# Half of one output-projection weight per layer to partitions 0 to 63, and a column of ones with step 0

## The chip, the cores and the metric

The kernel runs on one core of one Trainium2 chip. The metric is device time in microseconds, the median of several executions. A profiled execution is at hand too: its times, in us from the first instruction, are what "the profile" and "the trace" mean below.

The core's engines are PE (matrix multiply; PEld is its weight load), DVE (vector), ACT (scalar), POOL and SP. In this kernel all transfers are issued by SP's queue, and 16 DMA engines carry them.

## The reference

Two layers run over one token of width 640, each an attention block and then an MLP block. Attention has 32 heads of width 192 and looks at the last 4096 positions of a cache of keys and values, so that almost all of the bytes are cache. Both layers use the same weights and the same cache.

```python
def _A_ref(x, k_cache, v_cache, wq, wo):
    B, Sq, D = x.shape                     # 1, 1, 640
    Hq, Dh = 32, 192
    Hkv, Sk = k_cache.shape[1], k_cache.shape[2]      # 32, 32768
    W = min(4096, max(256, Sk // 4))                  # 4096
    q = (x @ wq) ...                                  # 32 heads of 192
    k, v = k_cache[:, :, Sk - W:, :], v_cache[:, :, Sk - W:, :]
    scores = einsum("bhqd,bhkd->bhqk", q, k) * Dh ** -0.5
    o = einsum("bhqk,bhkd->bhqd", softmax(scores), v)
    return o (as B, Sq, Hq * Dh) @ wo                 # wo: 6144 x 640

def _B_ref(x, w1, w2, w3, w4):
    hs = 0 for one token (every shifted block reads padding)
    x1 = x + hs
    return x1 + gelu(layernorm(x1) @ w3) @ w4         # 640 -> 1536 -> 640

x = A_x
for layer in range(2):
    x = x + _A_ref(layernorm(x), A_k_cache, A_v_cache, A_wq, A_wo)
    x = x + _B_ref(layernorm(x), B_w1, B_w2, B_w3, B_w4)
```

This is shortened; in the reference the two layers stand written out, and the shift by one or two positions in `_B_ref` is a pad and a slice, which for a sequence of one token leaves zeros.

## The kernel before

**Groups.** The 32 heads form eight groups of four (QH = 4). Layer 0 takes the groups from the last to the first, layer 1 from the first to the last (`GROUPS`). While group gi multiplies probabilities with values (`pv`), the keys of group gi+1 are turned around (`transpose_quart`, L377 on DVE) and scored (`scores`, L453 on PE).

**Transfers.** The big tiles are "cells", NCELL = 11 of them, each 128 partitions of 12,288 bytes: one K or V tile of one head (1536 KB) or one group's `wo` (960 KB). `layer_stream` writes out the order of all transfers for both layers, and `need` issues the next ones on SP's queue until the one asked for is out. So the order is fixed by hand: K and V tiles in turn, the `wo` of a group after its V tiles, at the end of a layer `w3` and `w4`. A transfer waits at SP until its cell is free, and until the eighth transfer before it has landed, as eight semaphores are used in turn. In layer 1 the turned keys of seven heads (NKEEP) and some values are still on chip from layer 0.

**One group's output.** `pv` accumulates a head's output in `O_ps` and DVE transposes it into `o_sb` (L576). `o_fold` sums it over partitions with the fold matrix `Lq` (L583, or L587 and L588 in the middle groups, `add=True`) and ACT scales it with the reciprocal of the softmax sum, `rl`, into the head's 32 partitions of `oT` (L584 or L589). So `oT` is 128 partitions (4 heads x 32) by NA = 6 columns, which is the layout that `load_wo` (L161 to L169) gives the group's rows of `wo`: partition p holds rows 6p to 6p + 5 of that group, one after another. `out_row` (L608) then multiplies `oT` with `wo` as a row: six columns by two halves of 320, L615. Groups at the ends of a layer use `out_proj` (L591, matmuls L597).

**Softmax sums.** `swap` multiplies `lh` with a 128 x 128 matrix of ones (L528, `l_ps`), so that each partition has the sums of the group's four heads; `recip` (L532) picks each partition's own with the mask `blkm` and inverts it. The same matrix of ones forms the sums of the layer norms (L325, L338, L681, L866, L868) and, as one element, of L501.

**Boundary of the layers.** After layer 0's last V tile come the last `pv`, `out_proj`, the norm sums, the products with `w3` (L901) and `w4` (L933), and then layer 1's norm and query projection. The cells that hold the old `w3`, `w4` and V are freed there, and layer 1's first new transfers wait for that.

Of the kernel before, what the change touches and what calls it, by code (L numbers as in the profile page):

```python
# [8 lines left out]
BF16 = mybir.dt.bfloat16  # L9
# [8 lines left out]
P = 128  # L18
# [17 lines left out]
def kernel(  # L36
# [26 lines left out]
    QH = 4  # L63
# [21 lines left out]
    assert W4C % 2 == 1 and W4C < NF  # L85
    GROUPS = [[list(range(h, h + QH)) for h in range(0, H, QH)] for _ in range(2)]
    GROUPS[0].reverse()

    head = ctx.enter_context(tc.tile_pool(name="head", bufs=1))
    fixed = ctx.enter_context(tc.tile_pool(name="fixed", bufs=1))  # L90
# [70 lines left out]
    def load_wo(layer, c):  # L161
        t = take(("wo", layer, c))
        src = A_wo[c * QC:(c + 1) * QC, :].rearrange("(p c) n -> p (c n)", c=NA)
        parts = {NG - 2: (3, 3), NG - 1: (3, 2, 1)}.get(c, (NA,)) if layer == 1 else (NA,)
        i = 0
        for n in parts:
            nc.sync.dma_start(t[:, i * D:(i + n) * D], src[:, i * D:(i + n) * D])
            i += n
        return t  # L169
# [91 lines left out]
        out=ident[:], in_=ident[:], compare_op=ALU.not_equal, fill=1.0,  # L261
        base=0, pattern=[[-1, P]], channel_multiplier=1,
    )
    ones = const.tile([P, P], F32, name="ones")
    nc.vector.memset(ones[:], 1.0)
    Lf = wx_sb[:, 0:2 * P].bitcast(F32).rearrange("p (j i) -> p j i", j=4)
    nc.gpsimd.memset(Lf, 0.0)
    for base in (0, -1, -64, -65):
# [22 lines left out]

    Lq = const.tile([P, 32], F32, name="Lq")
    nc.vector.reduce_sum(Lq[:], ident[:].rearrange("p (j a) -> p a j", j=4), axis=AX.X)
    eps1 = head.tile([P, 1], F32, name="eps1")
    nc.vector.memset(eps1[:], eps)

# [25 lines left out]
    def ln_center(x, rowsum):  # L322

        mean_ps = psm.tile([P, 1], F32, tag="psm")
        nc.tensor.matmul(mean_ps[:], lhsT=ones[:], rhs=rowsum[:, 0:1], start=True, stop=True)  # L325
        xc = big.tile([P, ND], BF16, name="xc")
        nc.vector.scalar_tensor_tensor(out=xc[:], in0=mean_ps[:, 0:1].broadcast_to([P, ND]), scalar=-1.0 / D,
                                       in1=x[:], op0=ALU.mult, op1=ALU.add)
        xcf = big.tile([P, ND], F32, name="xcf")
        nc.vector.scalar_tensor_tensor(out=xcf[:], in0=mean_ps[:, 0:1].broadcast_to([P, ND]), scalar=-1.0 / D,  # L330
                                       in1=x[:], op0=ALU.mult, op1=ALU.add)
        junk = sm.tile([P, ND], F32, tag="ln_junk")
        ssq = sm.tile([P, 1], F32, tag="ln_ssq")
        nc.scalar.activation(junk[:], xcf[:], ACTF.Square, accum_out=ssq[:, 0:1])

        def total():
            var_ps = psm.tile([P, 1], F32, tag="psm")
            nc.tensor.matmul(var_ps[:], lhsT=ones[:], rhs=ssq[:, 0:1], start=True, stop=True)  # L338
            return var_ps

        return xc, xcf, total
# [131 lines left out]
    def softmax_steps(n, ST_ps, sc):  # L473
        held = {}

        def part_max():
            pm = big.tile([P, 1], F32, name="pm")
            nc.vector.tensor_reduce(out=pm[:], in_=ST_ps, op=ALU.max, axis=AX.X)  # L478
            held["pm"] = pm

        def turn_max():
            pmT_ps = psm.tile([1, P], F32, tag="psm")
            nc.tensor.transpose(pmT_ps[0:1, :], held["pm"][:, 0:1], ident[:, :])
            held["pmT"] = pmT_ps

        def full_max():
            ngm = big.tile([1, 2 * QH], F32, name="ngm")
            nc.vector.tensor_reduce(out=ngm[:], in_=held["pmT"][0:1, :].rearrange("o (q x m) -> o x q m", q=4, m=NM),
                                    op=ALU.max, axis=AX.XY, negate=True)
            held["PrT"] = o_bytes[:, SW:2 * SW]  # L490

            wide = held["PrT"][0:1, :].bitcast(F32)
            nc.vector.tensor_scalar(
                out=wide.rearrange("o (q x m) -> o q x m", q=4, m=NM),
                in0=ngm[:].unsqueeze(1).unsqueeze(3).broadcast_to([1, 4, 2 * QH, NM]),
                scalar1=sc[0:1, 0:1], scalar2=None, op0=ALU.mult)
            held["w"] = wide

        def spread_max():
            nb_ps = psm.tile([P, 1], F32, tag="psm")  # L500
            nc.tensor.matmul(nb_ps[:], lhsT=held["w"],  # L501
                             rhs=ones[0:1, 0:1], start=True, stop=True)
            nb_sb = big.tile([P, 1], F32, name="nb_sb")
            nc.scalar.copy(nb_sb[:], nb_ps[:])  # L504
            Pr = o_bytes[:, 0:SW]
            lpart = big.tile([P, 1], F32, name="lpart")
            nc.scalar.activation(out=Pr, in_=ST_ps, func=ACTF.Exp,  # L507
                                 bias=nb_sb[:, 0:1], scale=sc[:, 0:1], accum_out=lpart[:, 0:1])
            held["Pr"], held["l"] = Pr, lpart

        def turn_p():
            nc.vector.transpose(held["PrT"], held["Pr"])  # L512
            lh = big.tile([P, QH], F32, name="lh")
            nc.vector.tensor_scalar(out=lh[:], in0=hm[:], scalar1=held["l"][:, 0:1], scalar2=None, op0=ALU.mult)
            held["lh"] = lh

        def swap():
            ng = NGK // NT
            PT_ps = psm.tile([P, n, NJ4, NGK], F32, tag="psm")
            src = held["PrT"].rearrange("p (g j i) -> p i j g", g=ng, j=NJ4)  # L520
            for m in range(NM):
                for q in range(NT):
                    nc.tensor.matmul(PT_ps[32 * m:32 * (m + 1), :, :, ng * q:ng * (q + 1)], lhsT=Eq[:, q, :],  # L523
                                     rhs=src[:, m:QW:NM], start=True, stop=True)
            PT = big.tile([P, n, NJ4 * NGK], BF16, name="PT")
            nc.scalar.copy(PT[:].rearrange("p h c -> p (h c)"), PT_ps[:].rearrange("p h j g -> p (h j g)"))  # L526
            l_ps = psm.tile([P, QH], F32, tag="psm")
            nc.tensor.matmul(l_ps[:], lhsT=ones[:], rhs=held["lh"][:], start=True, stop=True)  # L528
            held["lps"] = l_ps
            return PT  # L530

        def recip():  # L532
# [5 lines left out]
            return rl  # L538

        return part_max, turn_max, full_max, spread_max, turn_p, swap, recip  # L540

# [18 lines left out]
    def pv(layer, h, hq, PT, mid=None):  # L560
# [17 lines left out]
    def o_fold(h, oT, rl, add=False):  # L578
        r = slice(32 * (h % QH), 32 * (h % QH) + 32)
        oT_ps = psm.tile([P, NA], F32, tag="psm")  # L580
        if not add:
            for e in range(2):
                nc.tensor.matmul(oT_ps[r, :], lhsT=Lq[:], rhs=o_sb[:, e, :, e], start=(e == 0), stop=(e == 1))  # L583
            nc.scalar.activation(oT[r, :], oT_ps[r, :], ACTF.Copy, scale=rl[r, 0:1])  # L584
            return
        o2 = sm.tile([P, NA], F32, name="o2")
        nc.vector.tensor_add(o2[:], o_sb[:, 0, :, 0], o_sb[:, 1, :, 1])  # L587
        nc.tensor.matmul(oT_ps[r, :], lhsT=Lq[:], rhs=o2[:], start=True, stop=True)  # L588
        nc.scalar.activation(oT[r, :], oT_ps[r, :], ACTF.Copy, scale=rl[r, 0:1])  # L589

    def out_proj(layer, *terms):  # L591

# [15 lines left out]
    def out_row(layer, c, oT, acc, first):  # L608
# [1 line left out]
        wo_t = need("wo", layer, c)  # L610
        N = D // 2
        yr_ps = psm.tile([33, N], F32, tag="psm")
        for k in range(NA):
            for i in range(2):
                nc.tensor.matmul(yr_ps[32 * i:32 * i + 1, :], lhsT=oT[:, k:k + 1],  # L615
                                 rhs=wo_t[:, k * D + i * N:k * D + (i + 1) * N], start=(k == 0), stop=(k == NA - 1))
        give(("wo", layer, c))

        def add():
# [21 lines left out]
    def attention(layer, x_cur, rs_cur, x_new, z_new, rs_new, ss_new):  # L641
# [29 lines left out]
        def add_y(y_ps, n):  # L671
            y_new = x_new if n == 0 else sm.tile([P, ND], F32, name="y_acc")
            if n == 1:
# [4 lines left out]

                def center():
                    nm_ps = psm.tile([P, 1], F32, tag="psm")  # L680
                    nc.tensor.matmul(nm_ps[:], lhsT=ones[:], rhs=rs[:, 0:1], start=True, stop=True)  # L681
# [52 lines left out]
        for gi, cur in enumerate(groups):  # L734
            nxt = list(enumerate(groups[gi + 1])) if gi + 1 < len(groups) else []
            ST_n = None
            if nxt:
# [24 lines left out]
                else:  # L762
# [97 lines left out]
    def mixer(layer, x_cur, z, rs_cur, ss_cur, x_new, rs_new):  # L860
# [2 lines left out]


        s1_ps = psm.tile([P, 1], F32, tag="psm")
        nc.tensor.matmul(s1_ps[:], lhsT=ones[:], rhs=rs_cur[:, 0:1], start=True, stop=True)  # L866
        s2_ps = psm.tile([P, 1], F32, tag="psm")
        nc.tensor.matmul(s2_ps[:], lhsT=ones[:], rhs=ss_cur[:, 0:1], start=True, stop=True)  # L868
# [119 lines left out]
```

## Time and profile before

| | us |
|---|---|
| median of 3 runs | 520.23 (519.43 to 520.37) |
| the profiled execution's own time | 519.84 |
| its span, from the first to the last instruction | 518.0 |
| PE busy / DVE busy / ACT busy | 324.8 / 295.2 / 49.5 |
| data read | 216.47 MB, 418 GB/s over the span |

The profile's page gives busy time by engine, the span in 40 slices, the DMA queues, the chain of work that ended last, and the costliest groups of instructions. A group's line reads: source line, engine, operation, out<-in, count, then busy time and mean ns of one, then the idle time before them with what ended it. In the chain and the timeline the first number is the start and the second the length. Besides these answers the trace keeps one record for each DMA packet (queue, start, duration, size).

### The profile page before, as it was taken

Reading aid. Unit: us, or ns where it says so; the run is one execution under the profiler, and the core shown is the slowest. Engines: PE = TensorE matmul, PEld = TensorE weight load, DVE = VectorE, ACT = ScalarE, POOL = GpSimd, SP = SyncE. Lnnn points to the kernel's source line nnn. Section 1 sums busy time; section 2 is a strip of 40 time slices with the busy share of each in tenths; the row PEclk is TensorE's granted clock in tenths of the full one; section 3 lists DMA queues with packets and bytes.
Section 4 is the critical chain, followed back from the end, with each engine's and each line's share of the span. In section 5 each row is a group of like instructions: output and inputs, shape, how many; then the busy total and the mean of one; then the engine's idle time right before and its main releaser. Section 6 shows DMA issues by size and latency. Waiting matters only on the chain.

```text
span 518.0 us, 9589 instructions
## 1 busy us (share of the span) xinstructions
PE 324.8 (63%) x4146; PEld 192.6 (37%) x4146; DVE 295.2 (57%) x589; ACT 49.5 (10%) x175; POOL 4.0 (1%) x16
## 2 busy tenths in 40 slices
PE   2057656666664566767755866777566856648665
PEld 2024334333332334434333634434333433425334
DVE  2067667575584655656624356567675765664722
ACT  1000101010010100001011111001010101001011
POOL 2000000000000000000000000000000000000000
PEclk9999878565586755677665778557785676776855
DMA  8999999999999999999999999999999999999995
GB/s 347 433 425 426 433 426 427 432 428 425 433 426 427 431 426 429 428 426 431 424 425 396 385 426 429 428 428 428 429 426 427 432 428 426 426 434 426 427 416 235
DMA packets 23949, 217.08 MB, mean 419 GB/s; under 512 B 2532, under 2 KB 3044, under 8 KB 8420
## 3 DMA queue, kind: packets, MB, share of 16 engines
q1 hardware_dynamic: 23908, 216.48, 99.0%
q8 instruction: 32, 0.52, 0.4%
q14 instruction: 9, 0.07, 0.0%
HBM read 216.47 MB, written 0.00 MB: 418 GB/s over the span
## 4 chain that ended last, share of the span: by engine, by line
DMA 50%; PE 23%; DVE 22%; issue 2%; ACT 1%; SPq 1%; DVEq 0%; ACTq 0%
DMA cell<-in_A_k_cache_dram 39%; DVE cell L377 16%; DMA cell<-in_A_v_cache_dram 9%; PE ST_ps L453 9%; PE O_ps L569 7%; DVE o_sb L576 2%; DMA cell<-in_B_w_dram 2%; DVE pm L478 1%; PE nb_ps L501 1%; DVE o_sb L512 1%; ACT o_sb L507 1%; PE y_ps L637 1%; PE l_ps L528 1%; PE PT_ps L523 1%; PE qT_ps L407 1%
## 5 line engine op out<-in xcount | busy, mean ns | idle before, releaser
L453 PE MATMUL ST_ps<-cell,Qblk 128*16 128x256 bf16 x1536 | 163.7, 380 | 106.9 <-DVE cell L377 69.4
L377 DVE STREAM_TRANSPOSE cell<-cell 128x768 uint32<-128x768 uint32 x228 | 204.1, 945 | 15.2 <-DMA cell<-in_A_k_cache_dram 14.9
L453 PEld LDWEIGHTS <-Qblk 128*16 128x16 bf16 x1536 | 86.1, 111 | 176.5 <-issue 150.3
L569 PE MATMUL O_ps<-cell,PT 128*2 128x384 bf16 x1018 | 99.9, 461 | 8.2 <-DMA cell<-in_A_v_cache_dram 7.4
L576 DVE STREAM_TRANSPOSE o_sb<-O_ps 128x384 f32<-128x384 f32 x64 | 37.2, 581 | 111.8 <-PE O_ps L569 111.6
L569 PEld LDWEIGHTS <-PT 128*2 128x2 bf16 x1024 | 46.0, 100 | 22.1 <-issue 10.1
L512 DVE STREAM_TRANSPOSE o_sb<-o_sb 128x256 bf16<-128x256 bf16 x16 | 7.1, 446 | 33.2 <-ACT o_sb L507 24.2
L584 ACT ACTIVATE oT<-oT_ps,rl 32x6 bf16<-32x6 f32 x40 | 10.3, 258 | 164.0 <-PE oT_ps L583 157.8
L583 PEld LDWEIGHTS oT_ps<-o_sb,Lq 128*32 128x32 f32 x160 | 13.3, 145 | 19.3 <-issue 15.8
L583 PE MATMUL oT_ps<-o_sb,Lq 128*32 128x6 f32 x160 | 13.9, 195 | 10.4 <-DVE o_sb L576 9.9
L589 ACT ACTIVATE oT<-oT_ps,rl 32x6 bf16<-32x6 f32 x24 | 6.2, 258 | 107.6 <-PE ST_ps L453 87.1
L407 PE MATMUL qT_ps<-xc,wq_sb 128*128 128x1 bf16 x210 | 7.1, 165 | 12.8 <-DMA wq_sb<-in_A_wq_dram 12.0
L523 PE MATMUL PT_ps<-o_sb,Eq 128*32 128x32 bf16 x256 | 7.3, 237 | 9.3 <-DVE o_sb L512 4.1
L523 PEld LDWEIGHTS <-Eq 128*32 128x32 bf16 x256 | 5.4, 108 | 19.8 <-issue 19.7
L421 DVE TENSOR_TENSOR Xq<-qT_ps,maskq 128x24 bf16<-128x24 f32 (+1 forms) x18 | 2.8, 158 | 17.1 <-PE qT_ps L407 17.1
L396 PE MATMUL qr_ps<-wq_sb,xc 128*1 128x384 bf16 x90 | 12.1, 415 | 0.0
L407 PEld LDWEIGHTS <-wq_sb 128*128 128x128 bf16 x210 | 6.7, 102 | 14.0 <-DMA wq_sb<-in_A_wq_dram 13.0
L504 ACT COPY nb_sb<-nb_ps 128x1 f32<-128x1 f32 x16 | 2.5, 159 | 94.6 <-PE nb_ps L501 94.6
L615 PE MATMUL yr_ps<-cell,oT 128*1 128x320 bf16 x108 | 11.2, 355 | 0.0
L528 PE MATMUL l_ps<-lh,ones 128*128 128x4 f32 x32 | 7.7, 310 | 4.9 <-ACT PT L526 4.9
L428 PE MATMUL Qrep_ps<-Xq,Lb 128*128 128x24 bf16 (+1 forms) x18 | 3.2, 178 | 11.1 <-DVE Xq L421 10.8
L588 PE MATMUL oT_ps<-o,Lq 128*32 128x6 f32 x48 | 6.1, 199 | 6.5 <-DVE o L587 6.5
(143 smaller groups left out, 200.9 us busy)
## 6 DMA issues: line engine op xcount, KB each, us to landing
cell<-in_A_k_cache_dram SPq DMA_DIRECT2D x57, 1536.0 KB, 26.3
cell<-in_A_v_cache_dram SPq DMA_DIRECT2D x57, 1536.0 KB, 25.8
cell<-in_A_wo_dram SPq DMA_DIRECT2D x13, 960.0 KB, 26.5
wq_sb<-in_A_wq_dram SPq DMA_DIRECT2D x5, 1536.0 KB, 12.2
cell<-in_A_v_cache_dram SPq DMA_DIRECT2D x4, 768.0 KB, 23.8
cell<-in_A_v_cache_dram SPq DMA_DIRECT2D x2, 1248.0 KB, 11.5
cell<-in_B_w_dram SPq DMA_DIRECT2D x1, 1536.0 KB, 11.9
cell<-in_B_w_dram SPq DMA_DIRECT2D x2, 768.0 KB, 10.3
```

Source lines behind the costliest of these rows:

```text
L377: nc.vector.transpose(Tu, Ku[:, :, q * NY:(q + 1) * NY])
L396: nc.tensor.matmul(qr_ps[32 * i:32 * i + 1, :], lhsT=xc[:, kc:kc + 1], rhs=wq_sb[:, kc, t0 * P + i * N:t0 * P + (i + 1) * N], start=(kc == ...
L407: nc.tensor.matmul(qT_ps[:, tl:tl + 1], lhsT=wq_sb[:, kc, t * P:(t + 1) * P], rhs=xc[:, kc:kc + 1], start=(kc == 0), stop=(kc == ND - 1))
L453: nc.tensor.matmul(ST_ps[r:r + QW, :].rearrange("p (g i) -> p g i", g=ng), lhsT=Q[:, n, :], rhs=T4[:, :, f, :, t], start=(hq == 0 and n == ...
L512: nc.vector.transpose(held["PrT"], held["Pr"])
L523: nc.tensor.matmul(PT_ps[32 * m:32 * (m + 1), :, :, ng * q:ng * (q + 1)], lhsT=Eq[:, q, :], rhs=src[:, m:QW:NM], start=True, stop=True)
L528: nc.tensor.matmul(l_ps[:], lhsT=ones[:], rhs=held["lh"][:], start=True, stop=True)
L569: nc.tensor.matmul(O_ps[r:r + 2, :], lhsT=PT[:, hq, 2 * i:2 * i + 2], rhs=v_pair(V, h, 2 * i * Dh, 2 * Dh), start=(i < 4), stop=(i >= NB - 4))
L576: nc.vector.transpose(o_sb[:], O_ps.rearrange("p (e a c) -> p e c a", e=2, c=NA))
L583: nc.tensor.matmul(oT_ps[r, :], lhsT=Lq[:], rhs=o_sb[:, e, :, e], start=(e == 0), stop=(e == 1))
L584: nc.scalar.activation(oT[r, :], oT_ps[r, :], ACTF.Copy, scale=rl[r, 0:1])
L615: nc.tensor.matmul(yr_ps[32 * i:32 * i + 1, :], lhsT=oT[:, k:k + 1], rhs=wo_t[:, k * D + i * N:k * D + (i + 1) * N], start=(k == 0), stop= ...
```

## The change

In layer 0 the group of heads 16 to 19 and in layer 1 the group of heads 12 to 15 (the fourth in order, `SPLIT`) get their `wo` in another way. Columns 0 to 2 of the six go to 128 partitions as before, 480 KB. Columns 3 to 5, for all 128 rows, go to partitions 0 to 63 only: four transfers of 32 partitions each, 120 KB, two side by side in the free dimension. On the source side the 32 rows are written as 8 x 4, which puts them in another order in the 32 partitions.

`oT` grows to nine columns, the last six with 64 partitions in use. `o_fold_split` writes both parts: columns 0 to 2 with `Lq` to the head's own 32 partitions, columns 3 to 5 with a second fold matrix `Lp` (the new order of rows) to partitions 0 to 31 or 32 to 63. `recip_low` forms the reciprocals that belong to heads 2 and 3 on partitions 0 to 63. `out_row` has nine steps of two matmuls in that group, six of them over 64 partitions.

The matrix of ones becomes one column, read with step 0 along the other dimension.

```diff
+    SPLIT = [GROUPS[layer][3][0] // QH for layer in range(2)]
+    NH = NA // 2
...
     def load_wo(layer, c):
         t = take(("wo", layer, c))
         src = A_wo[c * QC:(c + 1) * QC, :].rearrange("(p c) n -> p (c n)", c=NA)
+        if c == SPLIT[layer]:
+            nc.sync.dma_start(t[:, 0:NH * D], src[:, 0:NH * D])
+            for g in range(4):
+                e = (NH + NH * (g // 2)) * D
+                nc.sync.dma_start(t[32 * (g % 2):32 * (g % 2) + 32, e:e + NH * D],
+                                  src[32 * g:32 * g + 32, NH * D:].rearrange("(b a) n -> a b n", b=4))
+            return t
...
-    ones = const.tile([P, P], F32, name="ones")
-    nc.vector.memset(ones[:], 1.0)
+    one = const.tile([P, 1], F32, name="one")
+    nc.vector.memset(one[:], 1.0)
+    ones = one[:, 0:1].broadcast_to([P, P])
...
+    Lp = const.tile([P, 32], F32, name="Lp")
+    nc.vector.reduce_sum(Lp[:].rearrange("p (a b) -> p a b", b=4),
+                         ident[:].rearrange("p (j b a) -> p a b j", j=4, b=4), axis=AX.X)
...
+        def recip_low():
+            lq = big.tile([P, QH], F32, name="lq")
+            rl = big.tile([P, 1], F32, name="rl_low")
+            nc.vector.scalar_tensor_tensor(out=lq[0:64, 0:2], in0=held["lps"][0:64, 2:4], scalar=1.0,
+                                           in1=blkm[0:64, 0:2], op0=ALU.mult, op1=ALU.mult, accum_out=rl[0:64, 0:1])
+            nc.vector.reciprocal(rl[0:64, :], rl[0:64, :])
+            return rl
...
+    def o_fold_split(h, oT, rl):
+        hq = h % QH
+        r, lo_, e = slice(32 * hq, 32 * hq + 32), slice(32 * (hq % 2), 32 * (hq % 2) + 32), NH + NH * (hq // 2)
+        oT_ps = psm.tile([P, NA + NH], F32, tag="psm")
+        o2 = sm.tile([P, NA], F32, name="o2")
+        nc.vector.tensor_add(o2[:], o_sb[:, 0, :, 0], o_sb[:, 1, :, 1])
+        nc.tensor.matmul(oT_ps[r, 0:NH], lhsT=Lq[:], rhs=o2[:, 0:NH], start=True, stop=True)
+        nc.tensor.matmul(oT_ps[lo_, e:e + NH], lhsT=Lp[:], rhs=o2[:, NH:],
+                         start=True, stop=True)
+        for at, i, s in ((r, 0, rl[0]), (lo_, e, rl[hq // 2])):
+            nc.scalar.activation(oT[at, i:i + NH], oT_ps[at, i:i + NH], ACTF.Copy, scale=s[at, 0:1])
...
     def out_row(layer, c, oT, acc, first):
-        for k in range(NA):
+        split = c == SPLIT[layer]
+        NK = NA + NH if split else NA
+        for k in range(NK):
+            p = P // 2 if split and k >= NH else P
             for i in range(2):
-                nc.tensor.matmul(yr_ps[32 * i:32 * i + 1, :], lhsT=oT[:, k:k + 1],
-                                 rhs=wo_t[:, k * D + i * N:k * D + (i + 1) * N], start=(k == 0), stop=(k == NA - 1))
+                nc.tensor.matmul(yr_ps[32 * i:32 * i + 1, :], lhsT=oT[0:p, k:k + 1],
+                                 rhs=wo_t[0:p, k * D + i * N:k * D + (i + 1) * N], start=(k == 0), stop=(k == NK - 1))
...
-                    rl = recip()
+                    rl = recip(cur[0] // QH == SPLIT[layer])
...
-            oT = sm.tile([P, NA], BF16, name="oT")
+            oT = sm.tile([P, NA + NH], BF16, name="oT")
```

More of the change, by code (lines that the diff above doesn't have):

```diff
@@ L324, in ln_center @@
         mean_ps = psm.tile([P, 1], F32, tag="psm")
-        nc.tensor.matmul(mean_ps[:], lhsT=ones[:], rhs=rowsum[:, 0:1], start=True, stop=True)
+        nc.tensor.matmul(mean_ps[:], lhsT=ones, rhs=rowsum[:, 0:1], start=True, stop=True)
         xc = big.tile([P, ND], BF16, name="xc")
@@ L337, in total @@
             var_ps = psm.tile([P, 1], F32, tag="psm")
-            nc.tensor.matmul(var_ps[:], lhsT=ones[:], rhs=ssq[:, 0:1], start=True, stop=True)
+            nc.tensor.matmul(var_ps[:], lhsT=ones, rhs=ssq[:, 0:1], start=True, stop=True)
             return var_ps
@@ L501, in spread_max @@
             nc.tensor.matmul(nb_ps[:], lhsT=held["w"],
-                             rhs=ones[0:1, 0:1], start=True, stop=True)
+                             rhs=one[0:1, 0:1], start=True, stop=True)
             nb_sb = big.tile([P, 1], F32, name="nb_sb")
@@ L527, in swap, with recip @@
             l_ps = psm.tile([P, QH], F32, tag="psm")
-            nc.tensor.matmul(l_ps[:], lhsT=ones[:], rhs=held["lh"][:], start=True, stop=True)
+            nc.tensor.matmul(l_ps[:], lhsT=ones, rhs=held["lh"][:], start=True, stop=True)
             held["lps"] = l_ps
             return PT
-        def recip():
+        def recip_low():
[5 more added lines that the diff above has]
+            return rl
+        def recip(low=False):
             lq = big.tile([P, QH], F32, name="lq")
@@ L537, in recip @@
             nc.vector.reciprocal(rl[:], rl[:])
-            return rl
+            return (rl, recip_low()) if low else rl
         return part_max, turn_max, full_max, spread_max, turn_p, swap, recip
@@ L576, in pv @@
         nc.vector.transpose(o_sb[:], O_ps.rearrange("p (e a c) -> p e c a", e=2, c=NA))
+    def o_fold_split(h, oT, rl):
[9 more added lines that the diff above has]
+            nc.scalar.activation(oT[at, i:i + NH], oT_ps[at, i:i + NH], ACTF.Copy, scale=s[at, 0:1])
     def o_fold(h, oT, rl, add=False):
+        if isinstance(rl, tuple):
+            o_fold_split(h, oT, rl)
+            return
         r = slice(32 * (h % QH), 32 * (h % QH) + 32)
@@ L583, in o_fold @@
                 nc.tensor.matmul(oT_ps[r, :], lhsT=Lq[:], rhs=o_sb[:, e, :, e], start=(e == 0), stop=(e == 1))
-            nc.scalar.activation(oT[r, :], oT_ps[r, :], ACTF.Copy, scale=rl[r, 0:1])
+            nc.scalar.activation(oT[r, 0:NA], oT_ps[r, :], ACTF.Copy, scale=rl[r, 0:1])
             return
@@ L588, in o_fold @@
         nc.tensor.matmul(oT_ps[r, :], lhsT=Lq[:], rhs=o2[:], start=True, stop=True)
-        nc.scalar.activation(oT[r, :], oT_ps[r, :], ACTF.Copy, scale=rl[r, 0:1])
+        nc.scalar.activation(oT[r, 0:NA], oT_ps[r, :], ACTF.Copy, scale=rl[r, 0:1])
     def out_proj(layer, *terms):
@@ L680, in center @@
                     nm_ps = psm.tile([P, 1], F32, tag="psm")
-                    nc.tensor.matmul(nm_ps[:], lhsT=ones[:], rhs=rs[:, 0:1], start=True, stop=True)
+                    nc.tensor.matmul(nm_ps[:], lhsT=ones, rhs=rs[:, 0:1], start=True, stop=True)
                     ym = big.tile([P, ND], F32, name="y_m")
@@ L865, in mixer @@
         s1_ps = psm.tile([P, 1], F32, tag="psm")
-        nc.tensor.matmul(s1_ps[:], lhsT=ones[:], rhs=rs_cur[:, 0:1], start=True, stop=True)
+        nc.tensor.matmul(s1_ps[:], lhsT=ones, rhs=rs_cur[:, 0:1], start=True, stop=True)
         s2_ps = psm.tile([P, 1], F32, tag="psm")
-        nc.tensor.matmul(s2_ps[:], lhsT=ones[:], rhs=ss_cur[:, 0:1], start=True, stop=True)
+        nc.tensor.matmul(s2_ps[:], lhsT=ones, rhs=ss_cur[:, 0:1], start=True, stop=True)
         def centred(dt, name):
```

## The prediction

> **What bounds the kernel now.** I read the 40 slices and the DMA rows of the page first.
>
> ```profile
> DVE  2067667575584655656624356567675765664722
> DMA  8999999999999999999999999999999999999995
> q1 hardware_dynamic: 23908, 216.48, 99.0%
> q8 instruction: 32, 0.52, 0.4%
> q14 instruction: 9, 0.07, 0.0%
> ```
>
> No compute engine is near full, while the 16 DMA engines are busy in every slice. Time is therefore bytes per DMA engine, and the latest engine decides. Besides the 216.48 MB of data the engines fetch instructions: 32 packets on q8, 9 on q14. The chain that ended last shows where the stream touches the computation: at the end of layer 0 and at the end of the kernel.
>
> ```profile
> 265.46 11.56 DMA cell<-in_A_v_cache_dram
> 277.06 0.81 PE O_ps L569 x8
> ...
> 500.70 10.35 DMA cell<-in_B_w_dram
> 511.10 0.50 PE V_ps L901 x12
> ...
> 513.94 1.22 PE y_ps L933 x40
> ```
>
> Each time a transfer's landing starts the last stretch of work, and a transfer has landed when its slowest engine has.
>
> The trace records start, duration, size and queue of each packet, not its engine. But a transfer of 128 partitions gives every engine the same list, and a packet follows the one before it on its engine within some ns, so I strung the packets into 16 chains. In the steady state a 12,288 B packet takes 456.5 ns, 7,680 B 287.1 ns, 3,840 B 145.9 ns, a completion 5.9 ns. A q8 fetch delays its engine by 1.42 us. The 32 fall on only eight engines, four each: two per layer. Five of the q14 fetches sit on one of the other engines, which I call V, at 0.84 us each (three in layer 0). Nothing else over 0.35 us breaks a chain between 30 and 280 us. Ends of the last packet of each layer's weights, in us:
>
> ```
>                                   layer 0           layer 1
> eight engines with q8 fetches     284.71-286.21     512.20-514.37
> engine V                          285.54            512.10
> seven others                      282.90-283.47     510.62-512.18
> ```
>
> So the eight are on average 2.3 and 1.9 us late: two fetches, less the other side's own. The others run dry after layer 0 until the first transfer of layer 1, which SP issues only after PE's L901:
>
> ```profile
> 283.69 3.39 SPq L145 DMA_DIRECT2D cell<-in_A_v_cache_dram  x2
> 291.01 2.94 SPq L132 DMA_DIRECT2D cell<-in_A_k_cache_dram  x2
> ```
>
> First byte 284.65, 0.96 us after issue.
>
> **The change, part by part.** *The split.* Each layer's wo of its fourth group goes half as before (8 packets of 3,840 B on each engine) and half as four transfers of 32 partitions. Which engines carry those, no row shows directly. The nearest is the x row of five partitions: its five packets lie on five engines, none of them among the eight with q8 fetches, V among them. The bounds are all 16 engines (nothing moves) and the fetching eight themselves (2.46 us later at the end). I take the eight without q8 fetches, by that row. Each of these gets 16 packets more where it had 8: 24 x 145.9 + 5 x 5.9 = 3.53 us instead of 8 x 287.1 + 5.9 = 2.30, so +1.23 per layer; the fetching eight get 8 x 145.9 + 5.9 = 1.17, so -1.13.
>
> Against the table: *layer 0.* V ends at 285.54 + 1.23 = 286.77, the fetching ones at 286.21 - 1.13 = 285.08. The last V-cache tile of the layer shows the same (276.69 on the latest fetching engine, 276.01 on V, 277.24 after), so the chain from 277.06 on, SP's issue at 283.69 and the first byte come 0.55 later, the byte at 285.20. Now the fetching eight also run dry there, by a few tenths. V never does. *Layer 1.* V carries both loads: 512.10 + 2.46 = 514.56. The seven start 0.55 later and get 1.23: at most 512.18 + 1.78 = 513.96. The fetching eight gain 1.13, gain some 0.3 from starting level and may lose up to 1.0 to a restart (below): 513.0 to 513.9 for the latest. The latest is V: 514.56 against 514.37, +0.2 us. The lag of the fetching eight is gone, but one engine of the receiving side has fetches of its own, and on it the move overshoots.
>
> [...]
>
> *SP and the queue.* Four more issues per layer, 0.33 to 0.50 us each by the SP rows, between issues 3.7 us apart. Completion semaphores are eight, taken in turn, so an issue waits for the landing of the eighth transfer before it. With five small ones in the ring, the K transfer behind the split in layer 0 is issued when an earlier V tile lands at 153.94 instead of at 140.06, and its first packet starts at 161.50: 7.6 us of queued work remain. In layer 1 it is 384.12 instead of 375.75, against 391.40: 7.3 us. Nothing runs dry, cost 0. Without that cover each us of late issue costs one.
>
> *PE, ACT, DVE.* Rows for the new work:
>
> ```profile
> L615 PE MATMUL yr_ps<-cell,oT 128*1 128x320 bf16 x108 | 11.2, 355 | 0.0
> L589 ACT ACTIVATE oT<-oT_ps,rl 32x6 bf16<-32x6 f32 x24 | 6.2, 258 | 107.6 <-PE ST_ps L453 87.1
> L588 PE MATMUL oT_ps<-o,Lq 128*32 128x6 f32 x48 | 6.1, 199 | 6.5 <-DVE o L587 6.5
> ```
>
> Per layer 6 x 355 = 2.1 us for the row product, four fold products of two passes, 8 x 199 = 1.6, four scalings, 4 x 258 = 1.0, and two small DVE steps (0.15 and 0.16 us). All lies in the fourth and fifth groups, where landed tiles wait behind 15 to 23 us of queue (issue to first packet); cost 0, at most 5.0 us a layer if that cover were gone. One DVE reduction at the start (0.37, as Lq's) and a smaller memset lie before the first K tile's landing at 25 us: 0.
>
> *Ones with step 0.* As weights they are loaded in l_ps, the norms and the mixer's sums. A load of step 0 isn't in the trace. Nearest rows: L901 loads w3 with step 2 at 106 ns, L933 loads w4 with step 1 at 104, so the step costs nothing: 0. Above: twice the 0.25 us of an f32 load at four loads in the last chain, 1.0 us, of which PE's wait of 0.9 for w3 before 511.10 hides nearly all. Below: no gain, as the same columns are loaded.
>
> The profiled execution took 519.84, 1.84 around the span of 518.0; the sum makes it 520.0. The median of the runs is 0.39 above it; I add the difference to the median: 520.4. A measurement of this kernel can tell about 0.2%, 1.04 us, from no change.
>
> **The rivals.** *Faster:* the receiving side has room after all. At 292.7 to 293.8 the eight engines without q8 fetches except V, all seven of them, lost 0.75 to 2.35 us at one K transfer after having run dry, and V lost 0.63 two us later. If these losses aren't repeated, the seven end near 512, the fetching ones at 514.37 - 2 x 1.13 = 512.1, and V at 514.56 - 0.63 = 513.9; with one of V's fetches fewer in the way (0.84) it is 513.1, a gain of 1.3: 518.9. It decides from there: with V later than 513.3 the gain stays under 1.04. The most is 2.26, both layers' relief. For it: lags of 2.3 and 1.9 fit a shift of 1.23 + 1.13. Against it: V's five fetches are in the chains.
>
> *Slower:* the overshoot is larger. What decides is the margin of the receiving engines to the latest fetching one: 0.67 us at the end of layer 0 and 2.19 at the end, against loads of 1.23 and 2.46. Where fetches cost 0.9 us rather than 1.42, or where the receiving engines lose more on restart, the margin is gone by about 0.85 us and the result is slower by 1.04; with no margin at all the two loads cost 2.46: 522.7. As a middle, 521.7. For it: seven engines did lose up to 2.35 to a restart, and after the change more engines run dry.
>
> *Not what it says:* the 32-row transfers use all 16 engines, which leaves only completions and smaller packets, under 0.1 us per layer: 520.3, inside the forecast's range.
>
> **How the numbers follow.** Forecast (V as the new latest, within 0.2%) 0.42 and the spread over 16 engines 0.08: same 0.50. The overshoot 0.28 slower. The room 0.22 faster. The forecast's own range is 519.5 to 521.3. The range for 8 in 10 reaches just past the faster case's 518.9, and above to 522.2, between the overshoot's middle and its full price.
>
> **What would show it.** Right: in the chains of the changed kernel 3,840 B packets 24 per layer on eight engines and 8 on the rest; V ends last; layer 1's first issue some 0.5 us later; no gap behind the split. Wrong: the fetching eight still last, or ending over 1 us sooner with V not in the way; 3,840 B packets alike on all 16; gaps in the DMA slices at 160 or 390 us; l_ps or s_ps loads longer than 0.25 us.

## The result and the profile after

The changed kernel takes 521.58 us in the median of 11 runs (521.02 to 522.42), the kernel before 520.23 us beside it (519.42 to 521.27). The ratio is 1.0027, with a 95% interval of 1.0017 to 1.0036: slower by 1.35 us. Forecast were 520.4 us, within 518.8 to 522.2, and "the same" as the likeliest. The time lies in the range, but the likeliest case did not come: the prediction took 0.2%, 1.04 us, for what can be told from no change, and 0.27% is above it (the interval begins a little below, at 0.17%). The profiled execution took 521.5 us, its span 519.6 (before 518.0).

The DMA rows of the page after, which answer to those shown of before:

```profile
DMA  8999999999999999999999999999999999999995
q1 hardware_dynamic: 24228, 216.48, 98.8%
q8 instruction: 33, 0.54, 0.4%
q14 instruction: 9, 0.07, 0.0%
```

The bytes are the same, the engines are as full as before, and there are 320 packets more, the small ones of the eight transfers. So the stream is as dense as it was, and it ends later. Next the chain that ended last, at the end of layer 0 and of the kernel (start, length, what):

```profile
265.83 11.86 DMA cell<-in_A_v_cache_dram
277.73 0.81 PE O_ps L592 x8
...
502.25 10.33 DMA cell<-in_B_w_dram
512.62 0.50 PE V_ps L942 x12
...
515.47 1.22 PE y_ps L974 x40
```

The last landing of layer 0 that the chain shows moved by 0.67 us (277.06 to 277.73), the landing of w3 at the end by 1.52 (511.10 to 512.62). SP's timeline shows the restart of the stream behind layer 0, and the splits themselves:

```profile
139.77 11.57 SPq L172 DMA_DIRECT2D cell<-in_A_wo_dram  x4
154.42 0.35 SPq L134 DMA_DIRECT2D cell<-in_A_k_cache_dram  x1
...
284.37 3.39 SPq L147 DMA_DIRECT2D cell<-in_A_v_cache_dram  x2
291.68 3.74 SPq L134 DMA_DIRECT2D cell<-in_A_k_cache_dram  x2
...
376.56 5.72 SPq L172 DMA_DIRECT2D cell<-in_A_wo_dram  x4
385.31 0.33 SPq L134 DMA_DIRECT2D cell<-in_A_k_cache_dram  x1
```

K behind the split is issued at 154.42 and 385.31 (forecast 153.94 and 384.12), and no slice of the DMA row drops there. Layer 1 restarts 0.68 us later (283.69 to 284.37; forecast 0.55).

Which engines took the load, the packet chains tell: 3,840 B packets of 149 ns, in both kernels, and those of the 32-row transfers on exactly eight engines. These are not the eight without q8 fetches. Six of the eight have none, V among them, and **two fetch instructions**. Ends of the last packet, from the chains, in us:

```
                                     layer 0             end
before   the two fetching engines    284.71, 285.67      513.11, 513.18
after    the same two, receiving     286.74, 286.86      515.56, 515.83
before   V                           285.54              512.10
after    V, receiving                286.73              514.56
before   six other fetching engines  285.63-286.21       512.20-514.37
after    six others, not receiving   284.95-285.49       514.02 at most
```

Chains can change places behind layer 0, where several engines stand still; a layer's ends are therefore put down by the fetches and transfers of that layer. The two in the first row can be told from the others in every profile: their q8 packets of 16 KB take 0.88 us, those of the six others 0.92 to 0.97 (1.02 against 1.06 to 1.11 in two padded kernels below; single packets take longer, as 1.33 us at 266.82 and 1.18 at 284.05 in the profile after). In the cycle of eight in which the fetches come they are always two neighbours, the fifth and sixth in the profile before, the second and third after. Which two places differs from program to program, and in every chain that shows both, these two also receive. The chains are sharp at the splits of the changed kernel: a packet of 3,840 B follows the one before it on its engine 3 to 4 ns before that one's recorded end, eight engines show 8 and then four times 4 of them, eight show 8 alone.

### The profile page after: what moved, and what is told of

It reads as the page before. It is cut to its first block, busy times and chain, and to the rows that moved or that the text cites. A ratio compares the mean times of both kernels' runs of the same rounds, so it can differ in the third digit from the quotient of the medians.

```text
span 519.6 us, 9673 instructions
## 1 busy us (share of the span) xinstructions
PE 333.5 (64%) x4174; PEld 196.1 (38%) x4174; DVE 294.8 (57%) x596; ACT 51.2 (10%) x183; POOL 4.0 (1%) x16
## 2 busy tenths in 40 slices
DMA packets 24270, 217.09 MB, mean 418 GB/s; under 512 B 2596, under 2 KB 3108, under 8 KB 8740
## 3 DMA queue, kind: packets, MB, share of 16 engines
q1 hardware_dynamic: 24228, 216.48, 98.8%
## 4 chain that ended last, share of the span: by engine, by line
PE 37%; DVE 30%; DMA 26%; issue 4%; ACT 2%; SPq 1%; DVEq 0%; ACTq 0%
DVE cell L392 22%; DMA cell<-in_A_k_cache_dram 17%; PE ST_ps L468 15%; PE O_ps L592 12%; DMA cell<-in_A_v_cache_dram 7%; DVE o_sb L599 3%; DMA cell<-in_B_w_dram 2%; PE l_ps L543 1%; PE PT_ps L538 1%; PE nb_ps L516 1%; PE qr_ps L411 1%; DVE o_sb L527 1%; DVE pm L493 1%; ACT o_sb L522 1%; PE y_ps L678 1%
## 5 line engine op out<-in xcount | busy, mean ns | idle before, releaser
L468 PE MATMUL ST_ps<-cell,Qblk 128*16 128x256 bf16 x1536 | 166.5, 391 | 103.9 <-DVE cell L392 68.7
L592 PE MATMUL O_ps<-cell,PT 128*2 128x384 bf16 x1018 | 104.9, 480 | 7.8 <-DMA cell<-in_A_v_cache_dram 7.1
L592 PEld LDWEIGHTS <-PT 128*2 128x2 bf16 x1024 | 47.9, 103 | 22.3 <-issue 12.3
L622 ACT ACTIVATE oT<-oT_ps,rl 32x6 bf16<-32x6 f32 x40 | 10.3, 259 | 163.4 <-PE oT_ps L621 156.8
L411 PE MATMUL qr_ps<-wq_sb,xc 128*1 128x384 bf16 x90 | 13.3, 448 | 0.0
L543 PE MATMUL l_ps<-lh,one 128*128 128x4 f32 x32 | 8.8, 345 | 4.9 <-ACT PT L541 4.9
L656 PE MATMUL yr_ps<-cell,oT 128*1 128x320 bf16 (+1 forms) x120 | 11.4, 332 | 0.0
L627 ACT ACTIVATE oT<-oT_ps,rl 32x6 bf16<-32x6 f32 x16 | 4.1, 259 | 73.3 <-PE ST_ps L468 62.2
L543 PEld LDWEIGHTS l_ps<-lh,one 128*128 128x128 f32 x32 | 7.4, 287 | 7.5 <-ACT PT L541 7.1
L516 PEld LDWEIGHTS nb_ps<-one,o_sb 1*128 1x128 f32 x32 | 7.0, 272 | 7.3 <-issue 5.5
```

What stands on the lines that cost most here:

```text
L411: nc.tensor.matmul(qr_ps[32 * i:32 * i + 1, :], lhsT=xc[:, kc:kc + 1], rhs=wq_sb[:, kc, t0 * P + i * N:t0 * P + (i + 1) * N], start=(kc == ...
L468: nc.tensor.matmul(ST_ps[r:r + QW, :].rearrange("p (g i) -> p g i", g=ng), lhsT=Q[:, n, :], rhs=T4[:, :, f, :, t], start=(hq == 0 and n == ...
L516: nc.tensor.matmul(nb_ps[:], lhsT=held["w"], rhs=one[0:1, 0:1], start=True, stop=True)
L543: nc.tensor.matmul(l_ps[:], lhsT=ones, rhs=held["lh"][:], start=True, stop=True)
L592: nc.tensor.matmul(O_ps[r:r + 2, :], lhsT=PT[:, hq, 2 * i:2 * i + 2], rhs=v_pair(V, h, 2 * i * Dh, 2 * Dh), start=(i < 4), stop=(i >= NB - 4))
L656: nc.tensor.matmul(yr_ps[32 * i:32 * i + 1, :], lhsT=oT[0:p, k:k + 1], rhs=wo_t[0:p, k * D + i * N:k * D + (i + 1) * N], start=(k == 0), s ...
```

## The experiments

The theory to test is *bytes per engine*: the two receiving engines that also fetch instructions carry all three loads and end last. Rivals: the four more issues and the later K; the work on PE, ACT and DVE or the ones with step 0; a one-off at the restart. Where a run below names a number of engines, it is the number of completions, packets of 4 B, that a transfer leaves: 16 for one of 128 partitions, five for x, whose five packets the chains find on five engines, and eight for a 32-row transfer of the change (the page after counts 2,596 packets under 512 B, the one before 2,532, so 64 more for eight such transfers), whose 3,840 B packets the chains find on eight.

**Ones alone.** The kernel before, with the ones as in the change.

```diff
-    ones = const.tile([P, P], F32, name="ones")
-    nc.vector.memset(ones[:], 1.0)
+    one = const.tile([P, 1], F32, name="one")
+    nc.vector.memset(one[:], 1.0)
+    ones = one[:, 0:1].broadcast_to([P, P])
```

> The kernel before with the column of ones read with step 0, and nothing else of the change. Theory (engines): no packet moves, ratio 0.9990 to 1.0010; the loads of the mixer's sums stay at 0.25 us each. Rival (step-0 weights): the median load of l_ps rose from 189 to 288 ns in the changed kernel; if that is the step, the ratio is up to 1.002 and the loads show it here too. If it is the lower granted clock of that execution (0.653 against 0.700), they don't.

Measured: 520.33 us, a ratio of 1.000 (0.999 to 1.001): the step costs nothing. The 32 loads of `l_ps` are 48 ns longer in this profile than before, those in the norms are not. First the groups before, then with the step:

```profile
L528 PEld LDWEIGHTS l_ps<-lh,ones 128*128 128x128 f32 x32 | 6.3, 245 | 7.5 <-ACT PT L526 7.1
L325 PEld LDWEIGHTS mean_ps<-rs,ones 128*128 128x128 f32 x4 | 1.0, 313 | 0.7 <-DVE xT L318 0.4 <-DVE x L940 0.3
```

```profile
L529 PEld LDWEIGHTS l_ps<-lh,one 128*128 128x128 f32 x32 | 7.5, 293 | 7.5 <-ACT PT L527 7.0
L326 PEld LDWEIGHTS mean_ps<-rs,one 128*128 128x128 f32 x4 | 1.0, 310 | 0.7 <-DVE xT L319 0.4 <-DVE x L941 0.3
```

But the 48 ns are not shown to come from the step. The run with the issues alone, below, has the matrix of ones without a step, and its loads are long as well:

```profile
L537 PEld LDWEIGHTS l_ps<-lh,ones 128*128 128x128 f32 x32 | 7.2, 280 | 7.5 <-ACT PT L535 7.1
```

With the step they take 249 ns in the run with layer 0 alone and 264 in the second profile of the change. The lengths go rather with the granted TensorE clock of the execution, the expectation's other rival: 245 to 265 ns in the seven profiles at 0.690 to 0.705 of full speed (one of them without the step), 267 to 293 in the five at 0.645 to 0.662. Two lie between: 280 ns at 0.685, in the run with the issues alone, and 249 at 0.679, in the one with the upper half, which does not fit.

**All 16 engines, the rows in their own order.** The 32-row transfers without the 8 x 4 order, which uses all 16 engines (and `Lq` for `Lp`).

```diff
-                                  src[32 * g:32 * g + 32, NH * D:].rearrange("(b a) n -> a b n", b=4))
+                                  src[32 * g:32 * g + 32, NH * D:])
```

> The four 32-row transfers keep their number, their size and their place, but the rows are in natural order (32 x 1920 on both sides, Lq in the place of Lp). Theory (engines): in the changed kernel the 3,840 B packets of the 32-row transfers lie on eight engines, two of which also take two PE instruction fetches per layer; these two carry both and end last (515.83 and 515.56 us, against 514.37 before). If the natural order lets the 32 rows go to all 16 engines, two packets each, every engine gets what it had, and the time is that of before within 0.3 us: ratio 0.9995 to 1.0010. Rival (queue and instructions): four more issues, a queue 7 us deep instead of 15 to 23, and 5 us of PE, ACT and DVE work per layer cost the time; then this kernel stays at 1.0027.

**The upper half.** The moved half goes to partitions 64 to 127.

```diff
-                nc.sync.dma_start(t[32 * (g % 2):32 * (g % 2) + 32, e:e + NH * D],
+                nc.sync.dma_start(t[64 + 32 * (g % 2):64 + 32 * (g % 2) + 32, e:e + NH * D],
```

> As the changed kernel, but the moved half goes to partitions 64 to 127. Theory (engines by number): the same eight engines carry it, whatever the partitions, the two PE-fetching ones among them end last again, ratio 1.0027 as the changed kernel, within 0.001. Rival (engines by partition): the other eight carry it, six of which fetch PE instructions twice per layer; then all six end some 2.4 us later and two engines of the first eight no longer do: about 1.004 or more, and the chains show six fetching engines with 24 small packets.

**One column as 4 x 8 rows.** One column is moved instead of three, the 32 rows ordered for four engines.

```diff
-    NH = NA // 2
+    MV = 1
+    NH = NA - MV
...
-                                  src[32 * g:32 * g + 32, NH * D:].rearrange("(b a) n -> a b n", b=4))
+                                  src[32 * g:32 * g + 32, NH * D:].rearrange("(b a) n -> a b n", b=8))
```

> One column of six is moved instead of three, and the 32 rows are written as 4 x 8 on the source side. Theory (number of engines by the slowest dimensions, 4 of the source): each 32-row transfer lies on four engines, eight packets of 1,280 B each; these four get 8 x 241 + 32 x 51.8 + 29 = 3.61 us per layer where they had 2.30, +1.31, all others -0.37. If no engine of the four fetches PE instructions and none carries the five q14 fetches, all fetching engines gain 0.37 per layer and the ratio is 0.9985 to 1.000; if the engine with five q14 fetches is among them it ends near 512.1 + 2.6 = 514.7, ratio 1.000 to 1.001. Rival (still eight engines): +0.4 per layer on two fetching engines, ratio 1.001 to 1.002.

None of the three came as expected: 526.82 us, 1.0132 (1.0114 to 1.0150); 528.57 us, 1.0160 (1.0146 to 1.0174); 522.82 us, 1.0052 (1.0038 to 1.0066). The GB/s rows of the first and the second show where:

```profile
GB/s 346 428 427 431 425 430 432 424 430 430 426 427 314 425 427 433 426 426 431 424 424 393 374 425 433 425 428 430 426 428 356 430 426 429 429 425 433 426 416 239
```

```profile
GB/s 345 430 430 426 425 432 431 426 432 425 431 427 310 430 425 432 430 423 429 427 418 389 374 425 429 429 429 424 431 426 321 426 428 430 430 426 428 429 416 225
```

The 13th and the 31st slice, one for each split, show 314 and 356, 310 and 321, where the changed kernel has 430 and 426: in the first run that is 13.1 us x (1 - 314/430) = 3.5 us, and 2.2 by the same working. The 3,840 B packets, 149 ns in the change, take 242 (median) and 291, and the slowest 12,288 B packets near them up to 708 and 871 (99th percentile) instead of 460. The completions show 16 engines for each 32-row transfer in the first run, 8 in the second, 4 in the third (2,661, 2,597 and 2,564 packets under 512 B). The ratio of the second would fit its rival ("about 1.004 or more"), but most of its loss lies in the two slices of the splits and not at the end, so that is not the rival's reason. These shapes differ from the change in the number of engines (16 and 4 where the change has 8) or in the partitions that they fill, and in them the stream is slower at the splits (391 and 401 GB/s in the same two slices of the third). It hid what these runs were made for, and needed a run of its own with eight engines again:

**Eight engines again, the rows in another order.** Two transfers of 64 partitions as 8 x 8 rows; heads keep columns of their own, so `oT` is wider.

```diff
-            for g in range(4):
-                e = (NH + NH * (g // 2)) * D
-                nc.sync.dma_start(t[32 * (g % 2):32 * (g % 2) + 32, e:e + NH * D],
-                                  src[32 * g:32 * g + 32, NH * D:].rearrange("(b a) n -> a b n", b=4))
+            for g in range(2):
+                e = (NH + NH * g) * D
+                nc.sync.dma_start(t[0:64, e:e + NH * D],
+                                  src[64 * g:64 * g + 64, NH * D:].rearrange("(b a) n -> a b n", b=8))
```

> [...] Bytes per engine alone: ratio 1.0027 (1.0015 to 1.004), packets of 3,840 B at 149 ns. [...]

Measured: 525.85 us, 1.0104 (1.0091 to 1.0118), the 512 packets of 3,840 B at the two splits, moved half or not, at 192 ns in the median and 306 at the 95th percentile. The price is paid in the same two slices:

```profile
GB/s 343 430 426 429 424 432 431 428 429 428 427 429 370 430 423 432 430 423 432 421 423 381 389 425 428 427 430 424 431 426 362 429 428 428 429 429 430 425 415 205
```

The bytes are those of the change and the completions show eight engines again (2,564 packets under 512 B, 32 more than before for four transfers); what differs is which of the partitions 0 to 63 a row goes to, two transfers instead of four, and beside the stream six more steps of the row product. That the eight are the same ones was not shown: where packets take longer, the chains aren't sharp. The 8 x 4 order is thus no detail: partition 4e + b of each 32 gets row 8b + e (e = 0 to 7, b = 0 to 3), and in this order the packets to the lower half take 149 ns. Why was not shown; the traces record neither engines nor partitions.

**The issues alone.** The kernel before, its second half of the same two wo sent as four transfers of 128 partitions and 960 B.

```diff
+        if c == SPLIT[layer]:
+            nc.sync.dma_start(t[:, 0:NH * D], src[:, 0:NH * D])
+            w = NH * D // 4
+            for g in range(4):
+                e = NH * D + g * w
+                nc.sync.dma_start(t[:, e:e + w], src[:, e:e + w])
+            return t
```

> The kernel before, with the moved half of each of the two wo sent as four transfers of 128 partitions and 960 B each, so that the number of issues is that of the change and every engine keeps its share. Theory (bytes per engine): no engine gets more, so the ratio is 1.000, between 0.999 and 1.001, and the last engine ends within 0.5 us of the kernel before. Rival (the four more issues, the completions and the later K issue cost the time): the ratio is that of the change, 1.0027, with a gap in the DMA slices behind the split.

Measured: 520.28 us, 1.0004 (0.9995 to 1.0014); the last engine ends at 514.45 (before 514.37). Issues, completions and the fuller ring cost nothing that shows.

**The load twice.** Two wo of each layer are split.

```diff
-    SPLIT = [GROUPS[layer][3][0] // QH for layer in range(2)]
+    SPLIT = [[GROUPS[layer][gi][0] // QH for gi in (2, 4)] for layer in range(2)]
...
-        if c == SPLIT[layer]:
+        if c in SPLIT[layer]:
```

> As the change, but two wo of each layer are split (third and fifth group instead of the fourth), so the eight receiving engines get the load twice. Theory (bytes per engine): the two receiving engines that also fetch instructions end 2 x 1.23 = 2.5 us later than with the change, near 518.3 us, and the ratio is 1.0027 + 2.5/520.2 = 1.0074 (1.006 to 1.009). Rival (the cost of the change is a one-off, such as the restart behind layer 0 or an odd execution): under 0.5 us more, a ratio of 1.0027 to 1.0037.

Measured: 524.12 us, 1.0073 (1.0060 to 1.0085), as the theory has it. The chain at the end:

```profile
505.10 10.34 DMA cell<-in_B_w_dram
515.48 0.49 PE V_ps L943 x12
...
518.32 1.22 PE y_ps L975 x40
```

The two last engines end at 518.45 and 518.69, 2.9 us behind those of the change, for 2.46 us of load more. A one-off would have given at most 0.5. The issues and the work on PE, ACT and DVE double in this run too; that the load is what counts is read from these two engines' ends.

**Layer 1 alone, and layer 0 alone.**

```diff
-    SPLIT = [GROUPS[layer][3][0] // QH for layer in range(2)]
+    SPLIT = [GROUPS[layer][3][0] // QH if layer in (1,) else None for layer in range(2)]
```

> As the change, but only the wo of layer 1 is split. Theory (bytes per engine, both layers add up on the receiving engines that fetch instructions): these end 1.23 us earlier than with the change, near 514.5 us, the end of layer 0 is that of the kernel before, and the ratio is between 1.000 and 1.0012. Rival 1 (all of the cost is made at the end of layer 0 and carried on): ratio 1.000 with the last landing as before. Rival 2 (all of it is made in layer 1): ratio 1.0027.

> As the change, but only the wo of layer 0 is split. Theory 1 (each layer's load is carried to the end, as the prediction has it for V): the receiving engines end 1.23 us later than before, and the ratio is 1.0010 to 1.0024. Theory 2 (the run with layer 1 alone cost 1.0031, so the dry spell behind layer 0 levels the engines and its load is forgotten there): only the later start of layer 1 stays, 0.3 to 0.7 us, and the ratio is 1.000 to 1.0013.

Measured: layer 1 alone 522.01 us, 1.0031 (1.0020 to 1.0042); layer 0 alone 521.31 us, 1.0020 (1.0011 to 1.0029). Together 0.51%, where both at once cost 0.27%. The second lies where theory 1 put it, the first where rival 2 did, and these contradict each other. The chains show a different last engine in each, so that both agreements are chance:

- Layer 0 alone: the two receiving fetching engines end at 514.53 and 515.00, that is 1.4 and 1.8 us above the 513.11 and 513.18 of before. But the last ones, at 515.46 to 515.61, are three fetching engines that received nothing. As the chains have it, they had finished layer 0 by 285.4, ran dry, and lost 1.7 to 2.0 us each in stalls near 294, at a K transfer; before, that loss had fallen on engines without fetches.
- Layer 1 alone: one engine ends at 516.58, all others by 514.64. It is the eighth of the cycle, which is one of the receiving two in this program. In the kernel before, the engine in that place of the cycle, another one, ended at 512.20, just as its last fetch came; here the fetch at 512.6 lies 4 us ahead of the end. The other of the two is within 514.64. This profile is of the slowest of the run's eight executions (522.68 us; median 522.01, lowest 521.04), so part of the excess may be its own.

**The change once more, and with the code moved.**

> The changed kernel once more. The q8 fetches of each profile so far come in a cycle of eight engines, and two neighbours of the cycle take 0.88 us for 16 KB where the six others take 0.92 to 0.97; in the chains these two are the fetching engines on the receiving side (second and third of the cycle in the profile after, eighth and first in the run with layer 1 alone). Theory (bytes per engine): the same two, and a ratio of 1.0027 (1.0017 to 1.0037). Rival (where the fetches fall changes from load to load of one program): another pair, and a ratio that differs by up to 0.002.

Measured: 521.75 us, 1.0026 (1.0017 to 1.0035), with the same two of the cycle (0.88 us) and ends of 515.84 and 516.03. The program has the same pair in both of its profiles.

For another pair, 24 tiny memsets on POOL were to move the program's code:

```diff
+    for _ in range(24):
+        pad = head.tile([P, 1], F32, name="pad", tag="pad")
+        nc.gpsimd.memset(pad[:], 0.0)
```

> The kernel with layer 1 alone, with 24 memsets of 128 x 1 added on POOL at the start, which move no data of the stream but may move the program's code to other places and so the fetches to other engines. If the pair of fetching engines on the receiving side sets the excess of that run (eighth and first of the cycle, the eighth with a fetch at 512.6 us, 4 us ahead of its end), another pair gives a last landing 0.7 to 1.4 us sooner and a ratio of 1.0010 to 1.0022. If the pair doesn't matter, or doesn't change, 1.0031 again (1.002 to 1.0042).

> The changed kernel with the same 24 memsets on POOL at the start. Bytes per engine with any pair but the eighth and first: 1.0027 (1.0017 to 1.0037). If the eighth of the cycle becomes a receiving one, its fetch near 512 us comes on top: 1.004 to 1.0055. The POOL work itself: 0, as it ends before the first K tile lands at 25 us.

Measured: 527.99 us, 1.0147 (1.0133 to 1.0160), and 528.60 us, 1.0160 (1.0146 to 1.0174). The pairs did change (second and third; fourth and fifth), but both runs became 6 to 7 us longer for another reason, so they don't tell the theories apart. The POOL memsets are over early, and the whole stream is slower (POOL's timeline and the GB/s row of the change with memsets):

```profile
3.87 3.37 POOL L311 MEMSET pad<- 128x1 f32 x21
```

```profile
GB/s 350 423 426 420 420 428 422 424 422 424 423 421 421 427 421 425 422 419 427 416 409 377 384 420 427 420 423 422 426 420 422 426 421 423 420 425 427 418 406 198
```

From the 2nd slice to the 20th it moves 416 to 428 GB/s, where the change moves 422 to 437. A 12,288 B packet takes 464 ns in the median and 471 at the 95th percentile, where both were 460. The pad tile is in a pool that the kernel opens ahead of that of the cells; that it moves the cells, and that this is the cause, was not shown.

## Why the prediction was right or wrong

**The failed step: which engines receive.** "I take the eight without q8 fetches, by that row." The x row has five packets and shows five engines; it says nothing on the other three, and two of these fetch. The step named the right bound ("the fetching eight themselves") and then set it aside whole, where the truth was two of the eight. With these two the prediction's own sum gives the result: 513.18 + 2 x 1.23 = 515.64 for the later one (515.83 measured), 1.27 us behind 514.37; added to 520.23 that is 521.5, against 521.58. That a 32-row transfer uses eight engines was the author's assumption too, which no row of before shows; the chains and the completions of the change do show eight. What the x row could not show is which engines fetch the program.

**The mechanism, the size and the rival.** An overshoot on the receiving side was the slower rival, at 521.7 in its middle; it won, with 0.28 against 0.50 for "same". That the time lies in the range at all is owed to the allowance for this rival: the forecast's own range, 519.5 to 521.3, ends below it. Its condition was put on margins ("the margin is gone") of engines without fetches. It was met by two engines whose margin to the latest fetching one was 1.2 us at the end, against a load of 2.46.

**The loads.** +1.23 on a receiving engine: V's layer 0 ends 1.19 later (286.73, forecast 286.77). V's end was forecast at 514.56 and is 514.56, and 514.92 in the second profile; so V is where it was put, but third from the last. -1.13 for a fetching engine that doesn't receive: their ends in layer 0, 284.95 to 285.49 where 285.08 was forecast for the latest; so the latest gained 0.72 us, not 1.13.

**The restart.** Three profiles with the split in layer 0 (the change twice, layer 0 alone) issue the first transfer of layer 1 at 284.37 to 284.57, four without it (before, ones, issues, layer 1 alone) at 283.69 to 284.14: 0.49 us later in the mean, forecast 0.55. For the relieved engines the text allowed "may lose up to 1.0" in the restart; with layer 0 alone it was 1.7 to 2.0 by the chains, enough to make three of them the last. In the change they lose 1.2 to 1.6 there too, but layer 1's relief of 1.13 hides it behind the two receiving engines. That fits costs of the layers that don't add up: the time is a maximum over engines, and each version has another engine on top. Why the stalls fall on one engine and not on another stays open.

**Costs put at 0.** Queue and issues: 1.0004 alone. Ones with step 0: 1.000 alone. The sign that was named against it, loads of `l_ps` longer than 0.25 us, did come (287 ns in the change), but the run with the issues alone, without the step, shows it too (280). PE, ACT and DVE: the groups of the change stay near or under the durations that were put in (258, 199 and 355 ns):

```profile
L611 ACT ACTIVATE oT<-oT_ps,rl 32x3 bf16<-32x3 f32 x12 | 2.7, 254 | 36.4 <-PE oT_ps L608 23.5 <-PE ST_ps L468 12.9
L608 PE MATMUL oT_ps<-o,Lp 128*32 128x3 f32 x16 | 2.0, 196 | 0.0
L656 PE MATMUL yr_ps<-cell,oT 64*1 64x320 bf16 x24 | 2.0, 295 | 0.0
```

That they cost nothing follows from the sums of the last engines, which need no further term; it wasn't tried by itself.

**Left open.** In the run with layer 1 alone the end of the engine that is eighth in the cycle would be 513.18 + 1.23 = 514.4 by the same sum, or 512.20 + 1.23 + 1.42 = 514.85 if one starts from the eighth place before and adds its fetch; 516.58 was measured. 1.7 to 2.2 us more are of the size of a loss in the restart, but the chains of that run aren't certain there. That the place of the code decides what the change costs, by up to a fetch at the end, is argued from the chains of several programs; no two runs differ in that alone.

No run beat the kernel before, and none points to a version that would: in every chain here that shows both, an 8 x 4 transfer reaches two fetching engines.

## What to carry to other kernels

Where every DMA engine is full (98.8 to 99.0% of the span here), a shift of load between engines pays only if it is known, engine by engine, who receives it and what else this engine fetches; a row that shows five of eight is a bound and not an answer. Sum each engine to its end, take the maximum, and do it again for every version, since costs of single parts need not add (0.20% and 0.31% alone, 0.27% together here). When a transfer is reshaped, the order and the place of its rows can cost more than its bytes: 0.27% in one shape here, 1.0 to 1.6% in three others. Look at the durations of the packets first; 149 ns in the cheapest shape stood against 192 to 291 in these three.

## What the hardware showed that was not expected

*A packet took twice as long when the kernel changed only the partitions.* In the 8 x 4 order to the lower half a packet of 3,840 B takes 149 ns; to the upper half 291 ns, and the 99th percentile of the 12,288 B packets near the splits went from 460 to 871. No run shows why, nor whether the same eight engines carried it.

*Fetches of instructions on q8 fall on eight of the 16 engines* in the chains (32 packets before, 33 after), and these lie unevenly: two of the receiving eight, six of the others. Which places of the cycle the two have differs from program to program (six pairs of neighbours in 13 programs), and was the same in both profiles of one.

*With 24 memsets of a small tile on POOL the packets were about 1% slower*, 460 to 464 ns in the median, and the kernel 6 to 7 us, about as much as the worst of the other shapes (7.0 us more than the change, for the upper half).
